# The first channel product of batches 6, 7 and of the tail chunk by seven block products in place of eight

## The chip, the cores and the metric

The kernel runs on one core of one Trainium2 chip. The metric is the device time of one launch in microseconds (us). "Before" is the kernel as it stands, "after" the kernel with the change below. Engines are named as the profile names them: PE (TensorE matmul), PEld (weight load of PE), DVE (VectorE), ACT (ScalarE), POOL (GpSimd), SP (SyncE, which here only issues DMAs).

## The reference

Attention by random features, then a mixer layer over its result; 8 batches of 576 rows and 512 channels:

```python
q_p, k_p = phi(q_s), phi(k_s)               # 8 heads, 128 features, exp
num = q_p @ (k_p^T v); den = q_p @ sum(k_p)
x   = num / den                             # [8, 576, 512]
h   = relu(x^T @ w_tok1) @ w_tok2           # over the 576 rows, 256 hidden
u   = x + h^T
out = u + relu(u @ w_ch1) @ w_ch2           # over the 512 channels, 1536 hidden
```

## The kernel before

Of each batch 512 rows are one block (c = 0 to 7); the 64 remaining rows of all eight batches are gathered into one more block of 512 rows, the tail chunk, c = 8 (`B`). A block passes through three stages. Attention (`attention`) makes the features, in four pairs of heads (hp = 0 to 3). Token mixing (`token_mix`) makes `u` and turns it by a DMA transpose issued by SP (L777) into `uT`, with the channels on the partitions; the tail chunk's `uTt` comes from four such transposes (L834). Channel mixing (`channel_mix`) multiplies `uT` by `w_ch1` (1536 hidden channels, twelve blocks `cb` of 128), applies relu into `r3`, and multiplies by `w_ch2`.

In the first channel product (L945) one block `cb` is four matmuls of 128x512 in one PSUM bank, one for each 128 input channels, and one relu of 128x512 on ACT or DVE (L268, L270) frees the bank. A block c has 48 such matmuls. The second product (`channel_out_fast`, L895) is done since batch 1 by Strassen's scheme in Winograd's form: the operands are cut into 2 x 2 quarters and seven products do the work of eight. It needs sums of quarters of `r3` (L273, eight per block, 128x768, on DVE) and sums of weights (L426, once); seven products O0 to O6 of twelve 128x256 matmuls write to three banks X, Y, Z; DVE reads them (L884) into the output tile `o` and adds `u`; two DMAs store it.

What runs when is written out by hand. Every piece of work is a job with a number. The list `ORDER` gives the order in which the jobs are issued; each engine takes its own jobs in that order, and waits only for what the job needs. `SLOT` says which of several equal buffers each job takes (the eight PSUM banks too): a job that takes a bank waits for the last reader of the bank's former content. `MOVED` sends a job to another engine than its usual one. The costs and keys of the jobs in the code do not enter a run.

Around the change the lists put work of two neighbouring batches between each other: while PE does the first channel product of batch 5, it also does attention of batch 6; the first product of 6 goes with attention and token mixing of 7; the first products of 7 and of the tail chunk stand together, with the second product of 7; the second product of the tail chunk ends the kernel.

The lines that the diff leaves alone but the prediction uses: L895 (matmuls of the second product), L945 (of the first), L884 (reads), L635, L647, L680, L713 (attention on PE), L722 and L723 (the attention result, two DVE instructions for each of eight heads), L659 (a DVE maximum).

## Time and profile before

| | |
|---|---|
| median of three runs | 281.75 us (281.57 to 281.98) |
| the profiled execution | 281.83 us, of which the span from the first to the last instruction is 280.0 us |
| granted TensorE clock, mean | 0.979 of full speed; 1.00 from 40 us on |
| PE busy | 267.5 us, 96% |
| DVE busy | 221.3 us, 79% |
| ACT busy | 141.1 us, 50% |
| POOL busy | 92.1 us, 33% |

Busy time is a share of the span. A matmul's own duration in the profile is longer than its distance from the next, because matmuls overlap in the array; the distance from start to start is what counts for the sum, and the chain view gives it (a piece of n matmuls, without the overlap of the last).

### The profile page before, as it was taken

How to read it: one execution, taken by the hardware profiler on the slowest of the kernel's cores; microseconds unless marked ns; L12 is line 12 of the kernel's file. 1: busy time of each engine (PE TensorE's matmuls, PEld its weight loads, DVE VectorE, ACT ScalarE, POOL GpSimd, SP SyncE). 2: the span in 40 equal slices, each digit the busy share in tenths (PEclk: the TensorE clock that was granted, in tenths of full speed). 3: DMA queues.
4: the chain of work that ended last, by engine and by line, in shares of the span. 5: the costliest groups of instructions: out<-in, count | busy, mean ns of one | idle time of the engine just before them, and what ended most of it. 6: DMA issues, size and time to landing. Idle time of an engine off the chain costs nothing.

```text
span 280.0 us, 6246 instructions
## 1 busy us (share of the span) xinstructions
PE 267.5 (96%) x2516; PEld 167.4 (60%) x2516; DVE 221.3 (79%) x457; ACT 141.1 (50%) x293; POOL 92.1 (33%) x116
## 2 busy tenths in 40 slices
PE   6579999999999999999999999999999999999993
PEld 2547545443657755665667546755675567456782
DVE  2598728499999799996997899977989595495583
ACT  2797993149676418743758445734764410033200
POOL 8587783007500971058008710510043000000001
PEclk9669999999999999999999999999999999999998
DMA  6999999999997999997989992960160324030125
GB/s 158 194 201 159 179 184 211 192 163 196 164 247 164 140 205 161 169 207 103 210 182 186 239 135 95 165 159 8 69 98 0 96 82 89 0 150 0 77 81 145
DMA packets 80524, 39.66 MB, mean 142 GB/s; under 512 B 63984, under 2 KB 76016, under 8 KB 80304
## 3 DMA queue, kind: packets, MB, share of 16 engines
q0 software_dynamic: 31744, 17.74, 44.2%
q1 hardware_dynamic: 46832, 15.77, 28.9%
q10 hardware_dynamic: 1920, 5.77, 5.5%
q8 instruction: 19, 0.31, 0.5%
q14 instruction: 9, 0.07, 0.1%
HBM read 35.95 MB, written 16.52 MB: 187 GB/s over the span
## 4 chain that ended last, share of the span: by engine, by line
PE 91%; DVE 4%; DMA 3%; SPq 0%; ACT 0%; issue 0%; DVEq 0%
PE bank L945 32%; PE bank L895 27%; PE bank L769 5%; PE bank L756 5%; PE bank L979 4%; PE bank L635 3%; DMA wc<-in_k_dram 3%; PE bank L647 3%; PE bank L713 3%; PE bank L680 2%; DVE km L659 1%; PE bank L823 1%; PE bank L795 1%; DVE kT L264 1%; PE bank L807 1%; PE bank L715 1%
## 5 line engine op out<-in xcount | busy, mean ns | idle before, releaser
L945 PE MATMUL bank<-uT,wc 128*128 128x512 f16 x376 | 90.0, 379 | 0.0
L268 ACT ACTIVATE r<-bank 128x512 f16<-128x512 f32 (+1 forms) x88 | 49.2, 603 | 81.0 <-PE bank L945 64.5
L273 POOL TENSOR_TENSOR vs<-v,vs 128x512 f16<-128x512 f16 x32 | 34.2, 1071 | 95.7 <-DVE vs L661 49.8
L945 PEld LDWEIGHTS <-wc 128*128 128x128 f16 x424 | 38.5, 98 | 38.8 <-issue 2.2
L493 ACT ACTIVATE qp<-bank 128x512 f16<-128x512 f32 x64 | 37.3, 627 | 8.8 <-PE bank L647 8.7
L895 PEld LDWEIGHTS <-r 128*128 128x128 f16 x384 | 36.7, 98 | 8.1 <-issue 1.0
L493 ACT ACTIVATE kp<-bank 128x512 f16<-128x512 f32 x64 | 36.7, 620 | 8.1 <-PE bank L635 8.1
L659 DVE TENSOR_REDUCE km<-kp 128x8 f16<-128x1024 f16 x32 | 38.6, 1206 | 0.6 <-ACT kp L493 0.4
L270 DVE TENSOR_SCALAR r<-bank 128x512 f16<-128x512 f32 (+1 forms) x38 | 24.9, 670 | 11.3 <-PE bank L945 6.7
L723 DVE TENSOR_TENSOR x<-bank,rc 128x320 f16<-128x320 f32 x62 | 30.5, 492 | 2.1
L895 PEld LDWEIGHTS <-S 128*128 128x128 f16 x288 | 28.0, 98 | 5.9 <-issue 0.4
L895 PE MATMUL bank<-T,r 128*128 128x256 f16 x192 | 23.8, 273 | 0.0
L895 PE MATMUL bank<-wc,r 128*128 128x256 f16 x192 | 23.6, 273 | 0.0
L895 PE MATMUL bank<-T,S 128*128 128x256 f16 x192 | 23.4, 273 | 0.0
L884 DVE TENSOR_TENSOR o<-u,bank 128x512 f32<-128x512 f16 x28 | 19.0, 678 | 4.5 <-PE bank L895 4.3
L884 DVE TENSOR_TENSOR o<-o,bank 128x512 f32<-128x512 f32 (+1 forms) x27 | 16.4, 618 | 7.6 <-PE bank L895 7.1
L924 POOL DMA_DIRECT2D out_dram<-o x2 | 1.3, 644 | 60.1 <-issue 60.1
L713 PEld LDWEIGHTS <-qp 128*128 128x128 f16 x256 | 13.7, 98 | 8.2 <-DVE kvsb L264 0.3
L772 DVE TENSOR_TENSOR u<-x,bank 128x512 f16<-128x512 f16 x28 | 17.7, 680 | 0.1
L713 PE MATMUL bank<-kvsb,qp 128*128 128x65 f16 x256 | 15.1, 193 | 0.1
L722 DVE RECIPROCAL rc<-bank 128x5 f32<-128x5 f32 x62 | 11.4, 184 | 4.2 <-PE bank L715 1.7
L769 PE MATMUL bank<-r,w 128*128 128x512 f16 x56 | 14.4, 381 | 0.0
(119 smaller groups left out, 378.9 us busy)
## 6 DMA issues: line engine op xcount, KB each, us to landing
out_dram<-o ACTq DMA_DIRECT2D x9, 512.0 KB, 2.7
q<-in_q_dram POOLq DMA_DIRECT2D x6, 576.0 KB, 9.7
wc<-in_moe_w_ch_dram POOLq DMA_DIRECT2D x4, 768.0 KB, 10.7
k<-in_k_dram POOLq DMA_DIRECT2D x6, 512.0 KB, 7.7
v<-in_v_dram POOLq DMA_DIRECT2D x6, 512.0 KB, 9.8
out_dram<-o SPq DMA_DIRECT2D x5, 512.0 KB, 4.8
r<-in_q_dram POOLq DMA_DIRECT2D x4, 288.0 KB, 6.7
v<-in_v_dram POOLq DMA_DIRECT2D x4, 256.0 KB, 8.7
```

Of the source, the lines that this page charges most:

```text
L268: nc.scalar.activation(out=out, in_=in_, func=AF.Relu)
L270: nc.vector.tensor_relu(out=out, in_=in_)
L273: (nc.gpsimd if eng == "POOL" else nc.vector).tensor_tensor(**kw)
L493: nc.scalar.activation(out=out, in_=in_, func=AF.Exp, bias=0.0, scale=1.0)
L659: nc.vector.reduce_max(out=mx, in_=kpv, axis=AX.X)
L713: nc.tensor.matmul(ps[:, k, j * 65 : (j + 1) * 65], st, s[:, i, 0 : D + 1], start=True, stop=True)
L723: nc.vector.tensor_tensor(out=t_x[place("x", b)][:, :, (2 * hp + hs[0]) * D : (2 * hp + hs[0] + n) * D].rearrange("p j (i d) -> p i j d", ...
L769: nc.tensor.matmul(ps, w2_of(tb, j), r1[:, tb, :], start=(tb == 0), stop=(tb == NT - 1))
L772: nc.vector.tensor_tensor(out=t_u[place("u", b)][:, j, :], in0=t_x[place("x", b)][:, j, :], in1=bank(n), op=ALU.add)
L884: nc.vector.tensor_tensor(out=o, in0=a, in1=ps, op=ALU.add)
L895: nc.tensor.matmul(ps[:, j * DH : (j + 1) * DH], a[:, cb, j * P : (j + 1) * P], w[:, cb, :], start=(bank_of(b, j0) not in held and j == j0 ...
L945: nc.tensor.matmul(ps, wc1[:, db, cb * P : (cb + 1) * P], moving(db), start=(db == 0), stop=(db == ND - 1))
```

## The change

For blocks 6, 7 and 8 (`FAST1 = 6`) the first channel product is done by the same seven-product scheme; `channel_in_fast` is new, and `channel_mix` calls it in place of the twelve plain blocks.

- The weights `wc1` are cut into quarters A11, A12, A21, A22; four sums of 128x1536 (named W.S1, W.S2, W.S4, W.S3 here) are made once, on DVE, in buffers of earlier batches; S3 overwrites A21.
- For each block four sums of 128x512 of quarters of `uT` (V1 to V4), on DVE.
- The hidden channels go in three pairs p = 0, 1, 2 of 128-blocks. For each pair there are seven products P1 to P7, each of four 128x256 matmuls into one of three banks X, Y, Z, and seven instructions of 128x512: `ka` copies X (after P1) into Y, so that P2 adds to it in PSUM; `y` is the relu of Y; `kb` and `kc` copy X after P6 and after P7 into 32-bit buffers in SBUF; `t22` (kc + Z after P5) and `t21` (kb + Z after P3) are sums on DVE into `r3`; `r` is the relu of X after P4. P2 and P6 need ka, P7 needs kb, P3 needs t22, P4 needs kc. Two quarters of `r3` then get their relu in place, in two parts each (1024 and 512 elements).
- In the second product of blocks 6 and 7 the read of X after O0 (DVE, adds `u`) becomes a copy of X into Y on ACT; O1 adds to it, and the read of Y adds `u`. The sums of `r3` come in parts of 128x1024 and 128x512 in place of two of 128x768.
- The lists: `ORDER` is as before up to the start of the first product of batch 5 (only the banks of some warm-up matmuls differ), and new from there. `SLOT` is new from the beginning, so that in the unchanged part of the order too the jobs take other banks. `MOVED` is new from job 727 on.

Read out job by job, the new list has PE at batch 5's first product (block C1 of batch b is b.C1) in this order: 6.kv@3, 7.kp@2, 7.kp@1, 7.kp@3, 6.kv@1, 6.n1@0, 5.C1.8, 6.n0@3, 6.n1@3, 5.C1.9, 5.C1.4, 6.n0@0, 6.n0@1, 5.C1.2, 6.n1@1, 5.C1.11, 7.kp@0, 7.kt, and then token mixing of 6 (kp, kt, kv, n are jobs of attention at L635, L530, L680 and L713, with the pair of heads behind @). DVE has meanwhile the eight results of batch 6's heads (L722, L723), with W.S1 after the second and W.S2 after the third; then five maxima of batch 7, four reads of token mixing, and W.S4 and W.S3 after them. The first products of batch 6 follow 5.O1, those of 7 follow 6.O0, and those of the tail chunk start after 6.O5, between the last products of 7. The last jobs of PE are 8.P4 of the three pairs and then the second product of the tail chunk alone.

```diff
--- before
+++ after
@@ ORDER (new from about its 880th entry on; up to there only the warm-up banks differ), SLOT (new throughout), MOVED (new from job 727) @@
...
@@ after MOVED @@
+FAST1 = 6
+def covered(name):
+    kind = name[0][0] if isinstance(name[0], tuple) else name[0]
+    if kind in ("X", "Y", "Z"):
+        return len(name) == 2
+    return kind in ("h2", "h3", "h4", "qp", "htt", "cX", "cY", "cZ") or kind == "h1" and name[1] > 0
+def seeded(name):
+    return name[0] == "cY" or name[0] == "Y" and len(name) == 2 and name[1] >= FAST1
@@ class Planner @@
         self.held = {}
+        self.whole = [False] * places["bank"]
...
                     assert i < self.places[tag] and not left.get(owner.get((tag, i)))
                     owner[tag, i] = (tag, name)
+                    if tag == "bank":
+                        assert self.whole[i] or not seeded(name)
+                        self.whole[i] = covered(name)
@@ shapes, homes and weight sums @@
+    A11, A21, A12, A22 = [wc1[:, 2 * k : 2 * k + 2, e * NH * P : (e + 1) * NH * P] for k in range(2) for e in range(2)]
+    S3 = A21
+    HOME = {1: "kT", 2: "qT", 4: "v"}
+    OF_V = {0: "kT", 1: "qT", 2: "v"}
+    def slot_of(tag):
+        t = {"kT": t_kT, "qT": t_qT, "v": t_v}[tag][place(tag, "W")]
+        return t if len(t.shape) == 2 else flat(t)
+    def S_of(n):
+        return S3 if n == 3 else slot_of(HOME[n])[:, 0 : 2 * NH * P].rearrange("p (k c) -> p k c", k=2)
+    def V_of(n):
+        return slot_of(OF_V[n])[:, 2 * NH * P : 2 * NH * P + 4 * P].rearrange("p (j k s) -> p j k s", j=2, k=2)
+    def s_of(c, p, x):
+        i = place("s", (c, p, x))
+        t = flat(t_r1[place("r1", "W")]) if i == 2 else flat(t_x[place("x", "W")])[:, 2 * SM * i : 2 * SM * (i + 1)]
+        return t.bitcast(FP32)
+    j_W = {}
+    def first_weights(plain):
+        for n, a, b, op in ((1, lambda: A21, lambda: A22, ALU.add), (2, lambda: S_of(1), lambda: A11, ALU.subtract),
+                            (4, lambda: A12, lambda: S_of(2), ALU.subtract), (3, lambda: A11, lambda: A21, ALU.subtract)):
+            e_w = "DVE"
+            def go_w1(n=n, a=a, b=b, op=op, e_w=e_w):
+                tt(e_w, out=S_of(n), in0=a(), in1=b(), op=op)
+            j_W[n] = add(e_w, 0.95, FAST1 - 0.2, go_w1, deps=[*j_wc1, *([j_W[n // 2]] if n in (2, 4) else [*j_W.values()]), *(plain if n == 3 else [])],
+                         take=[("x", "W"), ("r1", "W")] if n == 3 else [(HOME[n], "W")])
@@ channel_out_fast @@
-    def channel_out_fast(c, key, jr):
+    def channel_out_fast(c, key, jr, ready=None):
         def r3(i, e):
             return t_r3[place("r3", c)][:, NH * e : NH * e + NH, 2 * P * i : 2 * P * i + 2 * P]
         def s_of(i):
             return t_S[:, i - 1]
         sums = {}
-        for g in range(2):
-            part = slice(g * NH // 2, (g + 1) * NH // 2)
-            need = [jr[cb + NH * e] for cb in range(part.start, part.stop) for e in range(2)]
+        PARTS = (slice(0, 3), slice(3, 6)) if ready is None else (slice(0, 4), slice(4, NH))
+        if ready is None:
+            ready = {(i, e): [[jr[cb + NH * e] for cb in range(p.start, p.stop)] for p in PARTS] for i in range(2) for e in range(2)}
+        for g, part in enumerate(PARTS):
             steps = (
-                (1, lambda: (s_of(1), r3(1, 0), r3(1, 1)), ALU.add),
-                (3, lambda: (r3(1, 0), r3(0, 0), r3(1, 0)), ALU.subtract),
-                (2, lambda: (s_of(2), s_of(1), r3(0, 0)), ALU.subtract),
-                (4, lambda: (s_of(3), r3(0, 1), s_of(2)), ALU.subtract),
+                (1, lambda: (s_of(1), r3(1, 0), r3(1, 1)), ALU.add, [*ready[1, 0][g], *ready[1, 1][g]], ()),
+                (3, lambda: (r3(1, 0), r3(0, 0), r3(1, 0)), ALU.subtract, ready[0, 0][g], (1,)),
+                (2, lambda: (s_of(2), s_of(1), r3(0, 0)), ALU.subtract, ready[0, 0][g], (1,)),
+                (4, lambda: (s_of(3), r3(0, 1), s_of(2)), ALU.subtract, ready[0, 1][g], (2,)),
             )
+            if c < FAST1:
+                steps = tuple((i, what, op, [*ready[0, 0][g], *ready[0, 1][g], *need], after) for i, what, op, need, after in steps)
             prev = []
-            for k, (i, what, op) in enumerate(steps):
+            for k, (i, what, op, need, after) in enumerate(steps):
                 e_sum = "DVE"
-                def go(what=what, op=op, part=part, e_sum=e_sum, c=c, g=g, k=k):
+                def go_s(what=what, op=op, part=part, e_sum=e_sum, c=c):
                     o, a, b = what()
                     tt(e_sum, out=o[:, part], in0=a[:, part], in1=b[:, part], op=op)
-                job = add(e_sum, 0.5, key + KEYS["S"] + 0.1 * g + 0.01 * k, go, deps=[*need, *prev], take=[("S", c)])
+                job = add(e_sum, 0.5 if c < FAST1 else (0.61, 0.34)[g], key + KEYS["S"] + 0.1 * g + 0.01 * k, go_s,
+                          deps=[*need, *(prev if c < FAST1 else [sums[x][g] for x in after])], take=[("S", c)])
                 prev = [job]
                 sums.setdefault(i, []).append(job)
         ops = (
-            ("X", lambda: r3(0, 0), W11, []),
-            ("Y", lambda: r3(0, 1), W21, []),
+            ("X", lambda: r3(0, 0), W11, sum(ready[0, 0], [])),
+            ("Y", lambda: r3(0, 1), W21, sum(ready[0, 1], [])),
             ("X", lambda: s_of(2), T2, sums[2]),
             ("Z", lambda: s_of(1), T1, sums[1]),
             ("X", lambda: r3(1, 0), T3, sums[3]),
             ("Z", lambda: s_of(3), W22, sums[4]),
-            ("X", lambda: r3(1, 1), T4, sums[1]),
+            ("X", lambda: r3(1, 1), T4, [*sums[1], *sum(ready[1, 1], [])]),
         )
...
+        seed = c >= FAST1 and not tail
+        of_s = (2, 3, 4, 5, 6)
...
+                                             start=(bank_of(b, j0) not in held and j == j0 and cb == 0 and not (seed and k == 1)), stop=False, skip_group_check=True)
                     held[bank_of(b, j0)] = True
-                deps = [*need, *jr, *j_T, *j_wc2] + [outs[x, h] for x in ({2: ["sA"], 4: ["s2"], 5: ["22"], 6: ["s3"]}.get(k, []))]
...
+                if k == 0 and seed:
+                    e_a = engine("ACT", "DVE")
+                    def go_a(e_a=e_a):
+                        copy(e_a, bank(bank_of("Y", 0)), bank(bank_of("X", 0)))
+                    outs["sA", h] = add(e_a, 0.5, key + KEYS["c2"], go_a, deps=[j], take=[("bank", bank_of("Y", 0))])
+                elif k == 0:
                     outs["sA", h] = read(k, "X", 0, 0, True, [j], False, j0, j1)
                 elif k == 1:
-                    outs["11", h] = read(k, "Y", 0, 0, False, [j, outs["sA", h]], True, j0, j1)
+                    outs["11", h] = read(k, "Y", 0, 0, seed, [j, outs["sA", h]], True, j0, j1)
@@ new: channel_in_fast @@
+    plain = []
+    def channel_in_fast(c, key, jt):
+        def src():
+            return t_uT[place("uT", c)] if c < B else uTt
+        def u_of(k, i):
+            return src()[:, 2 * i : 2 * i + 2, 2 * k : 2 * k + 2, :]
+        v_of = V_of
+        own = [("uT", c)] if c < B else []
+        sums = {}
+        for n, what, op, after in (
+            (1, lambda: (v_of(0), u_of(0, 1), u_of(0, 0)), ALU.subtract, ()),
+            (2, lambda: (v_of(1), u_of(1, 1), v_of(0)), ALU.subtract, (1,)),
+            (4, lambda: (v_of(2), u_of(1, 0), v_of(1)), ALU.subtract, (2,)),
+            (3, lambda: (u_of(0, 1), u_of(1, 1), u_of(0, 1)), ALU.subtract, (1,)),
+        ):
+            e_sum = "DVE"
+            def go_u(what=what, op=op, e_sum=e_sum):
+                o, a, b = what()
+                tt(e_sum, out=o, in0=a, in1=b, op=op)
+            sums[n] = add(e_sum, 1.0, key - 0.2, go_u, deps=[*jt, *[sums[x] for x in after], *j_W.values()], take=[("V", c)], give=own)
+        ops = {
+            1: ("X", lambda: A11, lambda: u_of(0, 0), [], True), 2: ("Y", lambda: A12, lambda: u_of(1, 0), [], False),
+            6: ("X", lambda: S_of(2), lambda: v_of(1), [sums[2], j_W[2]], False), 5: ("Z", lambda: S_of(1), lambda: v_of(0), [sums[1], j_W[1]], True),
+            7: ("X", lambda: S3, lambda: u_of(0, 1), [sums[3], j_W[3]], False), 3: ("Z", lambda: S_of(4), lambda: u_of(1, 1), [j_W[4]], False),
+            4: ("X", lambda: A22, lambda: v_of(2), [sums[4]], False),
+        }
+        raw = {(i, e): [] for i in range(2) for e in range(2)}
+        for p in range(NH // 2):
+            at = key + 0.15 * p
+            def bank_of(b, p=p):
+                return ("c" + b, c, p)
+            def rows(i, e, p=p):
+                return t_r3[place("r3", c)][:, NH * e + 2 * p : NH * e + 2 * p + 2, 2 * P * i : 2 * P * i + 2 * P]
+            def seen(b, bank_of=bank_of):
+                return bank(bank_of(b)).rearrange("p (t s) -> p t s", t=2)
+            def product(n, deps, give=(), p=p, bank_of=bank_of, at=at):
+                b, a, moving, need, begin = ops[n]
+                def go_p(b=b, a=a, moving=moving, begin=begin):
+                    ps, m, a_ = bank(bank_of(b)), moving(), a()
+                    for t in range(2):
+                        cb = 2 * p + t
+                        for k in range(2):
+                            nc.tensor.matmul(ps[:, 2 * P * t : 2 * P * t + 2 * P], a_[:, k, cb * P : (cb + 1) * P], m[:, :, k, :],
+                                             start=(begin and t == 0 and k == 0), stop=False, skip_group_check=True)
+                j = add("PE", mm(4, 256), at, go_p, deps=[*jt, *j_wc1, *need, *deps], take=[("bank", bank_of(b)), ("r3", c)],
+                        give=[*([("V", c)] if n in (4, 5, 6) else own), *[(x, "W") for x in (*HOME.values(), "x", "r1")], *give])
+                j.heavy = True
+                return j
+            def kept(x, deps, give=(), p=p, seen=seen, at=at):
+                e_k = engine("ACT", "DVE")
+                def go_k():
+                    copy(e_k, s_of(c, p, x).rearrange("p (t s) -> p t s", t=2), seen("X"))
+                return add(e_k, 0.5, at, go_k, deps=deps, take=[("s", (c, p, x))], give=give)
+            def summed(x, b, i, e, deps, free, p=p, seen=seen, rows=rows, at=at, bank_of=bank_of):
+                def go_t():
+                    nc.vector.tensor_tensor(out=rows(i, e), in0=s_of(c, p, x).rearrange("p (t s) -> p t s", t=2), in1=seen(b), op=ALU.add)
+                j = add("DVE", 0.6, at, go_t, deps=deps, give=[("s", (c, p, x))] + ([("bank", bank_of(b))] if free else []))
+                raw[i, e].append(j)
+                return j
+            p1 = product(1, [])
+            e_a = engine("ACT", "DVE")
+            def go_a(e_a=e_a, bank_of=bank_of):
+                copy(e_a, bank(bank_of("Y")), bank(bank_of("X")))
+            ka = add(e_a, 0.5, at, go_a, deps=[p1], take=[("bank", bank_of("Y"))])
+            p2 = product(2, [ka])
+            p5 = product(5, [])
+            e_y = engine("ACT", "DVE")
+            def go_y(e_y=e_y, rows=rows, seen=seen):
+                relu_to(e_y, rows(0, 0), seen("Y"))
+            raw[0, 0].append(add(e_y, 0.5, at, go_y, deps=[p2], give=[("bank", bank_of("Y"))]))
+            p6 = product(6, [ka])
+            kb = kept("b", [p6])
+            p7 = product(7, [kb])
+            kc = kept("c", [p7])
+            t22 = summed("c", "Z", 1, 1, [kc, p5], False)
+            p3 = product(3, [t22])
+            summed("b", "Z", 1, 0, [kb, p3], True)
+            p4 = product(4, [kc])
+            e_r = engine("ACT", "DVE")
+            def go_r(e_r=e_r, rows=rows, seen=seen):
+                relu_to(e_r, rows(0, 1), seen("X"))
+            raw[0, 1].append(add(e_r, 0.5, at, go_r, deps=[p4], give=[("bank", bank_of("X"))]))
+        ready = {k: [raw[k][:2], raw[k][2:]] for k in ((0, 0), (0, 1))}
+        for i, e in ((1, 1), (1, 0)):
+            ready[i, e] = []
+            for g, part in enumerate((slice(0, 4), slice(4, NH))):
+                e_p = engine("DVE", "ACT")
+                def go_n(part=part, i=i, e=e, e_p=e_p):
+                    x = t_r3[place("r3", c)][:, NH * e + part.start : NH * e + part.stop, 2 * P * i : 2 * P * i + 2 * P]
+                    relu_to(e_p, x, x)
+                ready[i, e].append([add(e_p, (0.33, 0.2)[g], key + 0.4, go_n, deps=raw[i, e][2 * g : 2 * g + 2])])
+        return ready
@@ channel_mix @@
     def channel_mix(c, key, jt):
+        if c == FAST1:
+            first_weights(plain)
+        if c >= FAST1:
+            channel_out_fast(c, key, [], channel_in_fast(c, key, jt))
+            return
```

More of the change, by code (lines that the diff above doesn't have):

```diff
@@ L87, in key_of, with __init__ @@
     return NEAR.get(str(b), {}).get(name, KEYS[name])
+class Job:
+    def __init__(self, eng, cost, key, fn, deps, take, give, rows, wire):
+        self.eng, self.cost, self.key, self.fn = eng, cost, key, fn
+        self.deps, self.take, self.give = deps, take, give
+        self.rows, self.wire = rows, wire
+        self.end = None
+        self.heavy = False
+FAST1 = 6
[6 more added lines that the diff above has]
+    return name[0] == "cY" or name[0] == "Y" and len(name) == 2 and name[1] >= FAST1
 class Job:
@@ L123, in run @@
                 self.warm(-1 - n)
+                self.whole[-1 - n] = True
                 continue
@@ L139, in place, with engine @@
         return self.held[tag, name]
-    def engine(self, usual):
+    def engine(self, usual, *others):
         return MOVED.get(len(self.jobs), usual)
@@ L192 @@
     COUNT = {"qT": 3, "kT": 3, "v": 3, "vt": 2, "qp": 4, "kp": 4, "vs": 4, "qpt": 2, "kpt": 2, "vbd": 2,
[L193 removed]
+             "kvsb": 3, "ktt": 2, "x": 3, "r1": 3, "u": 3, "uT": 3, "r3": 2, "S": 1, "V": 1, "s": 3, "o": 2, "bank": 8}
     plan = Planner(COUNT)
@@ L694, in attention @@
                        give=[("kp", (b, hp)), ("vs", (b, hp)), ("kpt", b)] + ([("vbd", b)] if dma_in else []))
-            e_kv = engine("ACT" if b >= NPE or BY[("ko", "ko1")[b]][hp] == "A" else "DVE")
+            e_kv = engine(*("ACT", "DVE") if b >= NPE or BY[("ko", "ko1")[b]][hp] == "A" else ("DVE", "ACT"))
             def kv_out(hp=hp, n_kv=n_kv, e_kv=e_kv):
```

26 lines of the change are left out of this document (12 added, 14 removed), and 47 rows, old and new, of the table ORDER.

## Prediction

> **What bounds the kernel now.** I read the page first: its busy shares, and its chain of work that ended last.
>
> ```profile
> PE 267.5 (96%) x2516; PEld 167.4 (60%) x2516; DVE 221.3 (79%) x457; ACT 141.1 (50%) x293; POOL 92.1 (33%) x116
> ...
> PE 91%; DVE 4%; DMA 3%; SPq 0%; ACT 0%; issue 0%; DVEq 0%
> ...
> L945 PEld LDWEIGHTS <-wc 128*128 128x128 f16 x424 | 38.5, 98 | 38.8 <-issue 2.2
> ```
>
> PE is busy for 96% of the span and makes 91% of the chain. A busy share can hide waits, so I asked the windows view for the stretch that the change rewrites, from 178 us to PE's end.
>
> ```profile
> 178.00:275.60 97.60, 97.56 (x798) 63.90 (x795) 74.45 (x148) 33.03 (x66) 10.06 (x11) 1.00 0.28 74
> ```
>
> PE is busy for 97.56 of 97.60 us at full clock; DVE for 74.45, ACT for 33.03. So this stretch lasts as long as its matmuls, and less matmul time shortens it, if DVE and ACT keep pace. What a matmul costs is in the chain view (start, length, what).
>
> ```profile
> 237.37 13.81 PE bank L945 x64
> ...
> 265.08 10.49 PE bank L895 x96
> 275.60 0.42 DVE o L884
> ```
>
> 64 matmuls of 512 columns without a gap: 13.81/64 = 0.2158 us each. 96 of 256 columns: 10.49/96 = 0.1093 us each. A weight load takes 0.098 us (its row is above), less than the 0.1093 us, and lies beneath the matmul before it; so a doubled number of loads per column shows no cost in L895, which already works like this.
>
> **The matmuls removed.** A block had 48 matmuls of 512 columns, 48 x 0.2158 = 10.36 us. Now it has 3 pairs x 7 products x 4 = 84 matmuls of 256, 84 x 0.1093 = 9.18 us. Three blocks: 3 x 1.18 = **-3.55 us** on PE, which is the path. The weight loads go from 48 to 84 a block, hidden as said.
>
> **What DVE and ACT get.** Prices come from DVE's and ACT's groups, kept apart by shape (count, busy us, mean ns).
>
> ```profile
> L270 DVE TENSOR_SCALAR r<-bank 128x512 f16<-128x512 f32 x36 | 24.1, 683 | 10.5 <-PE bank L945 6.7 <-PE bank L756 3.5
> ...
> L884 DVE TENSOR_TENSOR o<-o,bank 128x512 f32<-128x512 f32 x21 | 14.0, 676 | 7.1 <-PE bank L895 6.6 <-issue 0.2
> ...
> L273 DVE TENSOR_TENSOR S<-S,r 128x768 f16<-128x768 f16 x16 | 8.8, 551 | 0.0
> ...
> L609 DVE COPY qpt<-qpt 128x512 f16<-128x512 f16 x1 | 0.3, 294 | 0.0
> ```
> ```profile
> L264 ACT COPY o<-bank 128x512 f32<-128x512 f32 x2 | 1.2, 604 | 1.4 <-PE bank L979 1.4
> ```
>
> And the weight sums for the second product, in DVE's timeline, with POOL's beside them:
>
> ```profile
> 55.70 0.95 DVE L426 TENSOR_TENSOR T<-wc 128x1536 f16<-128x1536 f16 x1
> 56.57 2.47 DVE L772 TENSOR_TENSOR u<-x,bank 128x512 f16<-128x512 f16 x4
> ...
> 64.55 1.81 DVE L426 TENSOR_TENSOR T<-wc 128x1536 f16<-128x1536 f16 x1
> ```
> ```profile
> 64.07 1.47 POOL L273 TENSOR_TENSOR vs<-v,vs 128x512 f16<-128x512 f16 x1
> ```
>
> Instructions overlap by a little, so the distance counts: four of L772 in 2.47 us with a length of 0.68 are 0.60 apart, and the sum at 55.70 is followed after 0.87. DVE gains, in the stretch: four W sums at 0.87 = 3.5; twelve V sums of 128x512, two thirds of the 0.551 of 128x768, 0.36 each = 4.3; eighteen t sums like `o<-o,bank`, at 0.60 = 10.8; eight copies or relus of the new scheme that MOVED gives to DVE, 4.8; eight of the twelve in-place relus. The trace has no such relu: the nearest row is the 16-bit copy of 512 in 0.294, the upper bound a two-operand sum at 0.36 for 512; so 0.3 for 512 and 0.6 for 1024, together 3.6, between 3.3 and 4.6. DVE loses sixteen plain relus (9.6) and two reads after O0 (1.2). Sum: +16.2, so 90.7 of some 94 us. DVE becomes nearly as full as PE. ACT has 55 of the new copies and relus and of batch 5's relus, at 0.604, where it had 32 relus: 33.03 + 23 x 0.604 = 47 of 94 us.
>
> [...]
>
> **What PE waits for.** I walked the new list from the point where it departs, with these prices, engine by engine. The first tight place is token mixing of batch 6, which needs all eight results of its heads. DVE there:
>
> ```profile
> 183.26 0.68 DVE L270 TENSOR_SCALAR r<-bank 128x512 f16<-128x512 f32 x1
> ```
> ```profile
> 189.37 0.19 DVE L722 RECIPROCAL rc<-bank 128x5 f32<-128x5 f32 x1
> ...
> 190.00 0.18 DVE L722 RECIPROCAL rc<-bank 128x5 f32<-128x5 f32 x1
> ```
>
> At 183.26 DVE comes to this part of the list in both versions; the relu of that row goes to ACT, and from there eight results at 0.63 (189.37 to 190.00) and two W sums at 0.87 end at 183.26 + 5.04 + 1.74 = 190.04. PE:
>
> ```profile
> 182.26 0.41 PE L680 MATMUL bank<-vs,kp 128*128 128x65 f16 x8
> ...
> 182.56 0.28 PE L713 MATMUL bank<-kvsb,qp 128*128 128x65 f16 x4
> ...
> 182.71 0.28 PE L713 MATMUL bank<-kvsb,qp 128*128 128x65 f16 x4
> ```
> ```profile
> 194.18 0.33 PE bank L635 x8
> ```
>
> From 182.26 it has five column blocks at 0.863, eight n at 0.15 (182.56 to 182.71), two kv at 0.30 (182.26 to 182.56), four kp at 0.33, and kt with half of that: 4.32 + 1.20 + 0.60 + 1.32 + 0.16 = 7.6, so 189.86. PE waits 0.2, with the hand-over **+0.3 us**. What is queued behind token mixing on PE (blocks of batch 5) waits with it.
>
> After that DVE runs without a pause to about 213 us and PE reaches each of its needs with little to spare. V1 and P1 of batch 6 need `uT`; its transpose is issued at 199.5 behind the last read of token mixing, and lands by
>
> ```profile
> DMA to landing us min/median/max: 4.3/5.3/5.7
> ```
>
> 205.2 at the latest; PE comes to 6.P1 at 205.3 to 205.5. One n of batch 7 finds its bank free 0.3 late; 5.O4 has its read 0.4 before PE is there, 7's token mixing its results 0.5 before. From 7.P1 on DVE has pauses again, and the slacks are 0.2 to 0.5: V3 and kb before 7.P7 (0.1), t22 before P3 (0.4), the copy in place of the read after O0 (0.60, with 0.06 for the hand-over) before O1 under three products, 3 x 0.437 = 1.31. The output buffers come free by stores with
>
> ```profile
> out_dram<-o SPq DMA_DIRECT2D x5, 512.0 KB, 4.8
> ```
>
> and 6's read of Y stands about there: up to 0.3 late. For these I take **+0.3 us** (nothing to 0.8).
>
> The new SLOT lets jobs of the unchanged part take banks nearer to their last reader. The reader's end before is set against PE's start, pair by pair. The worst is at 39.76, where a kv takes the bank that this exp leaves at 39.87:
>
> ```profile
> 39.12 0.75 ACT L493 ACTIVATE qpt<-bank 128x512 f16<-128x512 f32 x1
> ```
> ```profile
> 39.76 0.41 PE L680 MATMUL bank<-vs,kp 128*128 128x65 f16 x8
> ```
>
> That is 0.11, with 0.06 for the hand-over 0.17; ten others are below 0.15 and partly take the same shift: **+0.2 us** (0.1 to 0.5).
>
> **The sum.** PE's end: 275.60 - 3.55 + 0.3 + 0.3 + 0.2 = 272.85. After it the last read and store as before, 280.0 - 275.6 = 4.4: a span of 277.25. The profiled execution has 281.83 - 280.0 = 1.83 around its span, and lies 0.08 above the median of the runs: 277.25 + 1.83 - 0.08 = **279.0 us**, 2.75 less. What a measurement of this kernel can tell from no change is about 0.2%, 0.56 us.
>
> **Rivals.** (1) *DVE becomes the bound between 183 and 213 us.* For it: 90.7 of 94 us, and a first stretch without a pause. The W sums are its price: the row at 64.55 took 1.81 where that at 55.70 took 0.95, and POOL's sum at 64.07 ran beside it. If two of the four fall on one, 1.9 us go to PE: 280.9. Against it: in POOL's timeline the sums of batch 6 run before the W sums,
>
> ```profile
> 182.94 1.05 POOL L273 TENSOR_TENSOR vs<-v,vs 128x512 f16<-128x512 f16 x1 [0.93 <-PE bank L715]
> ```
>
> ending at 183.99, W.S1 beginning at 184.5. [...] Chance 0.15.
>
> (2) *Slower: the products wait for their copies.* 45 products (five of each of nine pairs) now need a read of their own bank, where a column block needed only a free bank. One copy is 0.604 with 0.06; between a product and the one that needs its copy the list has two products at least, 0.87, so a copy that starts at once is hidden, one that stands behind another on ACT or DVE isn't. If 45 products wait 0.1 us more each, that is 4.5 us: 283.5. It decides from 2.75/45 = 0.061 us on average. Against it: ACT is at half of its time, and the pairs are interleaved. Chance 0.12.
>
> (3) *The whole gain:* no wait of PE is new: 281.75 - 3.55 = 278.2. For it: before, PE has next to none. Chance 0.10.
>
> **How the numbers follow.** The forecast has 0.63 (278.2 to 279.9 by its bounds), rival 1 0.15 (279.9 to 281.5), rival 2 0.12, rival 3 0.10. The range 277.9 to 281.5 leaves out rival 2 and the far ends of the others. Faster by over 0.2%: 0.63 + 0.10 + most of rival 1 = 0.84; same: 0.05; slower: 0.11.
>
> **What would show it.** PE matmuls 2516 + 108 = 2624; 252 of 256 columns in the first product, 0.109 apart, and no group of 512 columns after batch 5's. DVE near 90 us busy from 178 us on. PE's idle time before token mixing of 6 at 0.3 us, ended by the head's result (L723). PE's end at 272.9 and 4.4 us after it. I'm wrong if products start more than 0.12 apart, if W sums take 1.8, or if idle times of PE ended by ka, kb or t22 add up to over 1 us.

## The result, and the profile after

The changed kernel takes 279.76 us (median of four runs, 279.37 to 279.81), the kernel before beside it 281.77 us: a ratio of 0.9926 with a 95% interval of 0.9908 to 0.9943. The gain is 2.0 us; 279.0 us, a gain of 2.75, was forecast. The profiled execution of the changed kernel has 279.72 us and a span of 277.9. Its page, first the engines, then the shares of the chain:

```profile
PE 265.6 (96%) x2624; PEld 179.5 (65%) x2624; DVE 233.7 (84%) x487; ACT 154.5 (56%) x318; POOL 91.6 (33%) x115
...
PE 88%; DVE 4%; DMA 3%; ACT 2%; issue 1%; ACTq 0%; DVEq 0%
```

The windows view of the rewritten stretch (start and end; its length; PE, PEld, DVE, ACT, POOL busy):

```profile
178.00:273.50 95.50, 94.65 (x908) 74.85 (x906) 86.93 (x178) 46.54 (x91) 9.51 (x10) 1.00 0.28 77
```

PE has 2624 matmuls, as worked out, but for the first time it is idle: 94.65 of 95.50 us, where before it was 97.56 of 97.60. DVE stands at 86.93 us, ACT at 46.54. Three pieces of the chain:

```profile
231.57 3.50 PE bank L1053 x32
...
264.34 9.21 PE bank L965 x84
273.57 0.42 DVE o L954
```

The new products run at 3.50/32 = 0.1094 us a matmul, like those of the second product (9.21/84 = 0.1096). PE ends at 273.57 where it ended at 275.60, 2.03 sooner, and what follows takes 4.4 us, as before. So the saving of 3.55 was there, and 1.5 of it was lost in waits. The waits view of PE from 178 us on lists three and no more (who waited for whom, us, times, longest); before, it lists none:

```profile
PE bank L965 <- DVE o L954: 0.5, 1, 0.5
PE bank L699 <- DVE x L787: 0.2, 1, 0.2
PE bank L1053 <- ACT bank L297: 0.2, 1, 0.2
```

PE's idle time counts there from the modelled end of a matmul, which lies behind its distance to the next: a 256-column matmul lasts 0.273 us and the next starts after 0.109 (512 columns: 0.379 and 0.216), so each bracket of one is 0.16 too small, and for the short matmuls of L699 it is 0.2. From start to start PE lost 0.43 us ahead of 7.kp@3, 0.32 ahead of 6.P6/1 and 0.61 ahead of 5.O5. Here they are in the timelines, in order of time, each with the instruction that it waits for (start, length, instruction, idle time before it):

```profile
183.54 0.49 DVE L787 TENSOR_TENSOR x<-bank,rc 128x320 f16<-128x320 f32 x1
184.09 0.40 PE L699 MATMUL bank<-omT,kT 64*128 64x128 f16 x8 [0.24 <-DVE x L787]
...
208.02 0.68 DVE L954 TENSOR_TENSOR o<-o,bank 128x512 f32<-128x512 f32 x1
208.73 0.57 ACT L297 COPY bank<-bank 128x512 f32<-128x512 f32 x1 [1.57 <-DVE o L954]
209.35 0.49 PE L1053 MATMUL bank<-qT 128*128 128x256 f16 x3 [0.16 <-ACT bank L297]
...
223.62 1.02 DVE L306 TENSOR_TENSOR S<-r,S 128x768 f16<-128x768 f16 x2
224.56 0.68 DVE L954 TENSOR_TENSOR o<-o,bank 128x512 f32<-128x512 f32 x1
225.29 0.38 PE L965 MATMUL bank<-wc,S 128*128 128x256 f16 x2 [0.45 <-DVE o L954]
```

From the end of a DVE or ACT instruction here to the start of what waits for it are 0.03 to 0.06 us; the forecast took 0.06 for the hand-over. First: 7.kp@3 takes the bank of 6.n1@2, whose result, the first of batch 6's eight, DVE reads until 184.04. Second: 6.ka/1 on ACT, idle for 1.57 us, waits for the bank that DVE reads in 5.r11 until 208.70, and 6.P6/1 waits for 6.ka/1; 5.r11 stands on DVE behind the new sums V1 and V2 of batch 6. Third: 5.O5 adds to the bank that 5.r22 reads, and 5.r22 stands on DVE behind the last two sums of batch 5 (5.s4). All three are ended by DVE, which runs without a pause around the second, from 199.6 to 210.3. The fourth loss is in the unchanged part of the order, between two attention products of batch 6 (PE's timeline, before and then after):

```profile
176.54 0.60 PE L647 MATMUL bank<-qT,omT 64*128 64x512 f16 x4
176.98 0.39 PE L635 MATMUL bank<-omT,kT 64*128 64x128 f16 x8
```
```profile
176.60 0.81 PE L711 MATMUL bank<-qT,omT 64*128 64x512 f16 x4
177.24 0.40 PE L699 MATMUL bank<-omT,kT 64*128 64x128 f16 x8
```

The four matmuls hold 0.64 us where they held 0.44: 0.20 lost between the second and the third, with other banks in the same order. What else stands between PE's matmuls are gaps of about 0.1 us (0.09 to 0.12), nearly all where the tile shape changes, mostly from 128 to 64 rows or back; they add up to 1.81 us before and 1.70 after. So -3.55 + 0.43 + 0.32 + 0.61 + 0.20 - 0.11 = -2.10, and the stretch from 176.5 us on is 2.09 shorter (below).

### The profile page after: what moved, and what is told of

Its sections match the earlier page's. It is cut to its first block, busy times and chain, and to the rows that moved or that the text cites. A ratio compares the mean times of both kernels' runs of the same rounds, so it can differ in the third digit from the quotient of the medians.

```text
span 277.9 us, 6547 instructions
## 1 busy us (share of the span) xinstructions
PE 265.6 (96%) x2624; PEld 179.5 (65%) x2624; DVE 233.7 (84%) x487; ACT 154.5 (56%) x318; POOL 91.6 (33%) x115
## 4 chain that ended last, share of the span: by engine, by line
PE 88%; DVE 4%; DMA 3%; ACT 2%; issue 1%; ACTq 0%; DVEq 0%
PE bank L965 25%; PE bank L1120 22%; PE bank L1053 9%; PE bank L833 5%; PE bank L820 5%; PE bank L1155 4%; PE bank L711 3%; PE bank L699 3%; DMA wc<-in_k_dram 3%; PE bank L777 3%; PE bank L744 2%; DVE o L954 1%; PE bank L887 1%; DVE x L787 1%; PE bank L859 1%; ACT qp L557 1%
## 5 line engine op out<-in xcount | busy, mean ns | idle before, releaser
L301 ACT ACTIVATE r<-bank 128x512 f16<-128x512 f32 (+1 forms) x82 | 46.3, 604 | 43.5 <-PE bank L1120 25.6
L1120 PE MATMUL bank<-uT,wc 128*128 128x512 f16 x280 | 67.9, 379 | 0.0
L557 ACT ACTIVATE qp<-bank 128x512 f16<-128x512 f32 x64 | 36.6, 624 | 8.0 <-PE bank L711 5.2
L723 DVE TENSOR_REDUCE km<-kp 128x8 f16<-128x1024 f16 x32 | 38.5, 1205 | 0.6 <-ACT kp L557 0.4
L999 POOL DMA_DIRECT2D out_dram<-o x1 | 0.7, 665 | 73.4 <-issue 73.4
L303 DVE TENSOR_SCALAR r<-bank 128x512 f16<-128x512 f32 (+1 forms) x26 | 17.1, 663 | 7.5 <-PE bank L820 4.9
L954 DVE TENSOR_TENSOR o<-u,bank 128x512 f32<-128x512 f16 x28 | 19.0, 679 | 2.8 <-PE bank L965 2.6
L954 DVE TENSOR_TENSOR o<-o,bank 128x512 f32<-128x512 f32 (+1 forms) x25 | 15.1, 612 | 2.7 <-PE bank L965 2.5
L711 PE MATMUL bank<-qT,omT 64*128 64x512 f16 x64 | 12.5, 410 | 1.7 <-ACT qT L297 1.7
```

What stands on the lines that cost most here:

```text
L301: nc.scalar.activation(out=out, in_=in_, func=AF.Relu)
L557: nc.scalar.activation(out=out, in_=in_, func=AF.Exp, bias=0.0, scale=1.0)
L711: nc.tensor.matmul(ps[e], omT[half[e]], t[half[e], 2 * hp : 2 * hp + 2, 0:R], start=True, stop=True)
L723: nc.vector.reduce_max(out=mx, in_=kpv, axis=AX.X)
L954: nc.vector.tensor_tensor(out=o, in0=a, in1=ps, op=ALU.add)
L1120: nc.tensor.matmul(ps, wc1[:, db, cb * P : (cb + 1) * P], moving(db), start=(db == 0), stop=(db == ND - 1))
```

## The experiments

Two theories stand against each other. *Local stalls*: PE is the bound, and DVE's order delays it in three places. *DVE is the bound*: its sum of work sets the end, the stalls are where this shows, and a new order only moves them. The first 176 us of a run shift by up to 0.4 us either way from run to run (the stretch starts between 176.02 and 176.76), so next to the median stands the stretch in the profiled execution from the first matmul of L711 (L647 before) after 176 us to the start of the last read (L954, L884); it agrees between two executions of the changed kernel to 0.01. Names of jobs stand beside the numbers in the diffs.

| run | median us | ratio to before, 95% | stretch us |
|---|---|---|---|
| before | 281.77 | | 99.06 |
| after | 279.76 | 0.9926 [0.9908, 0.9943] | 96.97 |
| e0, the change again | 279.34 | 0.9921 [0.9905, 0.9937] | 96.98 |
| e1, 5.s4 early | 278.96 | 0.9910 [0.9891, 0.9929] | 96.37 |
| e2, 5.r11 early | 279.84 | 0.9939 [0.9923, 0.9955] | 97.20 |
| e3, 7.kp@3 and two W sums late | 282.54 | 1.0032 [1.0016, 1.0048] | 100.02 |
| e4, no W sums | 279.24 | 0.9909 [0.9887, 0.9931] | 96.67 |
| e5, V sums on GpSimd | 281.49 | 0.9985 [0.9972, 0.9998] | 98.44 |
| e6, an eighth left out, no sums | 279.88 | 0.9934 [0.9911, 0.9956] | 96.85 |
| e7, 5.s4 and W.S4 late | 278.90 | 0.9898 [0.9877, 0.9919] | 96.41 |
| e8, 5.s4, V sums of 6 and 8 on GpSimd | 278.70 | 0.9902 [0.9886, 0.9918] | 96.05 |
| e9, another bank for 7.kp@3 | 279.47 | 0.9935 [0.9916, 0.9954] | 97.15 |
| e10, e8 and e9, W.S1 and W.S2 on GpSimd | 278.53 | 0.9888 [0.9874, 0.9902] | 95.72 |

The kernel before had medians of 281.56, 281.82 and 281.60 us beside e0 to e3, e4 to e7 and e8 to e10. The intervals of neighbours overlap; the small differences are read from the stretch and the stalls. A stretch is one execution, though, and it shows more than the medians: e1, e8 and e10 are 0.61, 0.93 and 1.26 us below e0 in the stretch and 0.38, 0.64 and 0.81 us in the median.

**e0, the change again.**

> The changed kernel once more, beside the three re-ordered ones, so that steps of 0.3 us can be read on one chip. Both theories: 279.76 us within 0.2, a gain of 2.0 on the kernel before. In the trace three stalls of TensorE that the kernel before has not: 0.43 us ahead of 7.kp@3 (184.1), 0.32 ahead of 6.P6/1 (209.4), 0.61 ahead of 5.O5 (225.3), and 0.20 ahead of 6.qp@1 (177.0). With 0.1 at changes of the tile shape all gaps after 176 add up to 3.26 us, against 1.81 before: 3.55 saved less 1.45 is the gain of 2.0 to 2.1.

279.34 us, 0.2 below what was expected, with before lower by 0.2 too. The three stalls are there with the same lengths.

**e1, the third stall.**

```diff
 ORDER
-..., 957, 968 (6.t22/0), 1101, 980, ..., 1003, 848 (5.s4g1), 861, 858 (5.r22), ...
+..., 957, 968 (6.t22/0), 844 (5.s4g0), 848 (5.s4g1), 1101, 980, ..., 1003, 861, 858 (5.r22), ...
```

> Same work; batch 5's two fourth sums (s4, 0.55 us each) are put on VectorE ahead of 6.t22/1, into its idle time at 214.2, and so no longer stand ahead of 5.r22, for which 5.O5 waits. Theory of local stalls (TensorE is the bound, three places of VectorE's order hold it up): 5.r22 starts at the end of 5.O3, some 0.9 us sooner, the 0.61 us ahead of 5.O5 shrink to 0.1, nothing behind it is late: 279.2 us (279.1 to 279.4). Rival (VectorE's sum of work is the bound, its order is not): the stall comes back elsewhere, 279.75 within 0.2.

```profile
214.02 1.02 DVE L306 TENSOR_TENSOR S<-r,S 128x768 f16<-128x768 f16 x2
...
223.49 0.69 DVE L954 TENSOR_TENSOR o<-o,bank 128x512 f32<-128x512 f32 x1
```

In DVE's timeline the two sums stand in the former pause, 5.r22 starts at 223.49 and not at 224.56, and 5.O5 has no idle time before it. The stretch is 0.61 shorter, just the stall: local stalls hold here. The median, 278.96 us, lies 0.14 below the expected range.

**e2, the second stall by order.**

```diff
 ORDER
+..., 716, 852 (5.r11), 973, 1072 (7.no1@1), 1100 (7.no1@3), 727, 959, 955 (6.V1), 853, 960 (6.ka/0), 974 (6.ka/1), ..., 975 (6.P2/1), 964 (6.P6/0), ...
-..., 956 (6.V2), 852 (5.r11), ..., 974 (6.ka/1), ..., 964 (6.P6/0), ..., 978 (6.P6/1), 965, 1056, 975 (6.P2/1), ...
```

> Same work; 5.r11 (0.68 us on VectorE, frees the bank that 6.ka/1 fills) goes ahead of 7.no1@1, 7.no1@3 ahead of 6.V1, and 6.P2/1 ahead of 6.P6/0 on TensorE, so that V2 has 0.4 us more. Local stalls: the 0.32 us ahead of 6.P6/1 go, nothing new waits: 279.45 us (279.35 to 279.6). Rival, VectorE full from 178 to 210: the wait moves to 6.P6/0 for V2 or to 7.n0@2 for its bank, 279.75 within 0.2.

```profile
209.74 0.49 DVE L787 TENSOR_TENSOR x<-bank,rc 128x320 f16<-128x320 f32 x1
210.29 0.28 PE L777 MATMUL bank<-kvsb,qp 128*128 128x65 f16 x4 [0.32 <-DVE x L787]
```

The 0.32 us are gone, and 0.48 stand ahead of 7.n1@0, whose bank DVE reads until 210.23: the stretch grows by 0.22. The rival is right at this place, though the new wait is none of those that it named. DVE has no pause here, and this order only moved the wait.

**e3, the first stall by order.**

```diff
 ORDER
-..., 1087 (7.kp@3), 903 (6.kv@1), 1089, 951 (W.S1), 893 (6.n1@0), 827 (5.C1.8), ..., 952 (W.S2), ...
+..., 903 (6.kv@1), 827 (5.C1.8), 893 (6.n1@0), 1087 (7.kp@3), 1089, ..., 1093 (7.km@3), 951 (W.S1), ..., 952 (W.S2), 953 (W.S4), ...
```

> Same work; on TensorE 7.kp@3, which waited 0.43 us for a bank, goes behind 6.kv@1, 5.C1.8 and 6.n1@0, and W.S1 and W.S2 (0.95 us each) leave VectorE's queue ahead of the last head results of batch 6: S1 behind 7.km@3, S2 ahead of W.S4. Local stalls: token mixing of batch 6 starts 0.3 to 0.4 us sooner (190.2 for 190.57) and the end follows: 279.4 us (279.3 to 279.6). Rival: with VectorE's work only put off, the 0.4 us come back at 6.P6/0 or 6.P6/1, where VectorE is late already: 279.75 within 0.2, with a gap ahead of 6.P6/1 of 0.7.

```profile
186.47 0.28 PE L777 MATMUL bank<-kvsb,qp 128*128 128x65 f16 x4 [0.69 <-ACT kp L557]
...
210.92 0.68 DVE L954 TENSOR_TENSOR o<-o,bank 128x512 f32<-128x512 f32 x1
211.63 0.57 ACT L297 COPY bank<-bank 128x512 f32<-128x512 f32 x1 [1.89 <-DVE o L954]
212.26 0.49 PE L1053 MATMUL bank<-qT 128*128 128x256 f16 x3 [0.60 <-ACT bank L297]
```

Both were wrong, 3.2 us slower. The edit was bad in itself: a kp that comes 1.3 us later has its exp later, and 6.n0@3 waits 0.88 us (from start to start) for that bank. The last rows fit the rival's part: with the W sums put off, the stall ahead of 6.P6/1 is 0.77 us, as it said (0.7). Six more waits of 0.2 to 0.4 us from start to start came up, which were not taken apart.

**e4, without the sums of the weights.**

```diff
             def go_w1(n=n, a=a, b=b, op=op, e_w=e_w):
-                tt(e_w, out=S_of(n), in0=a(), in1=b(), op=op)
+                pass
```

> The changed kernel with the four sums of the weights left out (3.8 us of VectorE, S1 and S2 at 184.6 and 186.1, S4 and S3 at 200.1 and 200.9); the products read what lies in their places. It prices the terms of 0.3 us for token mixing of batch 6, and tells whether VectorE's work bounds the kernel. Theory of local stalls: 7.kp@3 still waits 0.43 us (6.no1@2 stands ahead of the sums), token mixing of 6 starts where it did, only the 0.32 us ahead of 6.P6/1 go: 279.0 to 279.1 where the change had 279.34 in the last call. Rival, VectorE's work is the bound between 178 and 210: 1 us or more comes back: 278.3 or less.

PE's waits:

```profile
PE bank L965 <- DVE o L954: 0.5, 1, 0.5
PE bank L699 <- DVE x L787: 0.2, 1, 0.2
```

3.8 us less on DVE give PE 0.3: the stretch is 0.31 shorter than in e0. The median, 279.24 us, is above the expected range, and far from the rival's. The stall ahead of 6.P6/1 is gone, the others stay. So the sums cost what one stall costs; DVE's sum of work isn't the bound of the whole stretch, and the stall ahead of 7.kp@3 is not of their making.

**e5, the V sums on GpSimd.**

```diff
-            e_sum = "DVE"
+            e_sum = "POOL"
             def go_u(what=what, op=op, e_sum=e_sum):
```

> The changed kernel with the twelve V sums of batches 6, 7 and the tail (128x512, 0.42 us on VectorE) on GpSimd, where such a sum takes 1.07 us in the profile of before. Theory (each V chain is 1.9 us longer, VectorE has 4.2 us less): 6.P6/0 late by 0.4 to 0.9, 7.P5/2 by 0.1, 8.P6/0 by 0.9, less the 0.32 us that 6.P6/1 waited: 0.5 to 1.5 us slower than the change, 280 to 281. Rival 1 of the prediction (VectorE's sums that run beside GpSimd's take twice as long, 1.8 for 0.95 us, as the T sums did): several us, 282 or more. If VectorE's sum of work were the bound: faster, 278 to 279.

DVE in the changed kernel beside the same jobs of batch 7:

```profile
229.40 0.49 DVE L303 TENSOR_SCALAR r<-r 128x512 f16<-128x512 f16 x2
229.92 0.42 DVE L306 TENSOR_TENSOR S<-r 128x512 f16<-128x512 f16 x1
230.26 0.42 DVE L303 TENSOR_SCALAR r<-r 128x1024 f16<-128x1024 f16 x1
```

With the V sums on GpSimd, DVE, GpSimd's two of these and PE behind them:

```profile
228.57 1.46 DVE L303 TENSOR_SCALAR r<-r 128x512 f16<-128x512 f16 x2
230.06 1.33 DVE L306 TENSOR_TENSOR S<-r 128x512 f16<-128x512 f16 x1
231.31 1.37 DVE L303 TENSOR_SCALAR r<-r 128x1024 f16<-128x1024 f16 x1
...
229.95 1.15 POOL L306 TENSOR_TENSOR v<-uT,qT 128x512 f16<-128x512 f16 x1
231.06 1.33 POOL L306 TENSOR_TENSOR uT<-uT 128x512 f16<-128x512 f16 x1
...
234.78 0.38 PE L1053 MATMUL bank<-uT,wc 128*128 128x256 f16 x2 [1.62 <-ACT bank L297]
```

Four DVE instructions that take 1.33 us together (0.49 + 0.42 + 0.42) take 4.16; the last three end 0.15 to 0.3 us after a sum of GpSimd ends. 6.s1g0 and 6.r11 come later by that, 7.ka/0 with them, and PE waits 1.78 us from start to start; with the stall ahead of 6.P6/1 gone, the stretch is 1.46 longer. 281.49 lies between the theory and rival 1: the price is rival 1's, but PE pays it in one batch of three. In the tail one relu of 128x512 takes 1.21 us too, beside V4 (246.89 to 248.05), and PE isn't late:

```profile
246.99 1.21 DVE L303 TENSOR_SCALAR r<-r 128x512 f16<-128x512 f16 x1
```

Around the V sums of batch 6 DVE reads PSUM, and its reads and head results keep 0.68 and 0.49 us (DVE, then GpSimd):

```profile
205.68 0.68 DVE L954 TENSOR_TENSOR o<-o,bank 128x512 f32<-128x512 f32 x1
...
206.49 0.49 DVE L787 TENSOR_TENSOR x<-bank,rc 128x320 f16<-128x320 f32 x1
...
205.64 1.16 POOL L306 TENSOR_TENSOR qT<-uT,kT 128x512 f16<-128x512 f16 x1
206.75 1.16 POOL L306 TENSOR_TENSOR uT<-uT 128x512 f16<-128x512 f16 x1
```

The relus of batch 7, with one input, grew about as much as the sum with two (0.42 to 1.37 and 0.42 to 1.33 us); by what mechanism, the runs don't show.

**e6, the saving without its price.** The kernel before, 18 of 144 matmuls left out.

```diff
-                for db in range(ND):
-                    nc.tensor.matmul(ps, ..., start=(db == 0), stop=(db == ND - 1))
+                nd = ND - 1 if c >= 6 and cb % 2 else ND
+                for db in range(nd):
+                    nc.tensor.matmul(ps, ..., start=(db == 0), stop=(db == nd - 1))
```

> The kernel before with the last of the four matmuls left out in every second column block of the first product of batches 6, 7 and the tail: 18 of 144, an eighth of 128x512, and no sums at all. It is the saving without its price. If TensorE bounds all of the last third: 18 x 0.2158 = 3.88 us less, 281.6 - 3.9 = 277.7 (277.5 to 278.0). Rival: relus and bank turnover take over in part when the four matmuls of a block become three: 278.5 or more.

```profile
215.72 0.28 PE L713 MATMUL bank<-kvsb,qp 128*128 128x65 f16 x4 [0.58 <-DVE kvsb L264]
...
251.88 0.50 PE L895 MATMUL bank<-T,S 128*128 128x256 f16 x3 [0.76 <-DVE S L273]
```

The rival's time is right; what PE waits for is a cast and a sum on DVE, not a relu or a bank itself. Of 3.88 us the stretch keeps 99.06 - 96.85 = 2.21: two waits for DVE, 0.75 and 0.92 us from start to start, come up in a kernel whose PE had been idle for 0.04 us of 97.60. This order feeds PE just in time and has hardly any slack; a faster PE alone runs into the engine that fed it. Ahead of both waits DVE runs with hardly a pause, from 212.7 to 215.7 and from 247.5 to 251.8; whether its load there or the place of the two jobs in its queue decides, this run doesn't tell.

**e7, work put off into the pause.** W.S4 goes with 5.s4; W.S3 and the V sums wait only for the sum that they need.

```diff
 ORDER
-..., 950, 1095, 824, 953 (W.S4), 1090, ..., 856, 1070, 957 (6.V4), 968 (6.t22/0), 1101, ..., 844, 1003, 848, 861, ...
+..., 950, 1095, 824, 1090, ..., 856, 1070, 953 (W.S4), 957 (6.V4), 968 (6.t22/0), 844, 848, 1101, ..., 1003, 861, ...
-... [j_W[n // 2]] if n in (2, 4) else [*j_W.values()] ...
+... [j_W[n // 2]] if n in (2, 4) else [j_W[1]] if n == 3 else [] ...
-... deps=[*jt, *[sums[x] for x in after], *j_W.values()] ...
+... deps=[*jt, *[sums[x] for x in after], *([j_W[n]] if n != 3 else [])] ...
```

> The changed kernel, same work: batch 5's fourth sums into VectorE's idle time at 214 as in the run before, and W.S4 too, from 200.1 to just ahead of 6.V4 (213.2), with the V sums waiting only for the weights' sum whose place they share. VectorE's full stretch ahead of 6.P6/1 is 0.87 us shorter. Local stalls: both the 0.61 us ahead of 5.O5 and the 0.32 ahead of 6.P6/1 go: 278.4 (278.2 to 278.6), 0.5 to 0.9 less than the change. Rival: work that is put off on VectorE comes back as a wait at 6.P4/1, 6.P7/1 or 6.P3/0 between 214 and 219: 279.0 or more.

```profile
216.12 0.70 DVE L297 COPY bank<-bank 128x512 f32<-128x512 f32 x1
216.87 0.60 PE L1053 MATMUL bank<-qT 128*128 128x256 f16 x4 [0.21 <-DVE bank L297]
```

Both stalls are gone, and a new one of 0.37 us stands ahead of 6.P6/2, for whose copy 6.ka/2 DVE comes too late. The stretch, 96.41, is that of e1 (96.37), and 278.90 us lies between the two forecasts. The rival is right in kind: the work that was put off comes back between 214 and 219, at a product that it did not name. The pause at 214 has no room for both.

**e8, the V sums of 6 and of the tail on GpSimd.** e1's order, and

```diff
-            e_sum = "DVE"
+            e_sum = "DVE" if c == 7 else "POOL"
             def go_u(what=what, op=op, e_sum=e_sum):
```

> The changed kernel with batch 5's fourth sums moved to 214 (as before), and the V sums of batch 6 and of the tail on GpSimd, those of batch 7 on VectorE. In the run with all twelve on GpSimd a stall of 1.78 us came up in batch 7 alone, where VectorE's in-place relus and S sums took 1.2 to 1.4 us beside GpSimd for 0.28 to 0.42; beside the V sums of 6 VectorE reads PSUM and was not slower. Theory (the price is the doubling of VectorE's SBUF work, and it falls where such work stands beside GpSimd): no stall in batch 7, none ahead of 6.P6/1 or 5.O5: 0.9 us below the change, 278.3 to 278.6. Rival (GpSimd's sums themselves are late, 1.15 us against 0.42): the stall of 0.4 to 0.9 ahead of 6.P6/0 or 8.P6/0, 279.0 or more.

```profile
PE bank L699 <- DVE x L787: 0.2, 1, 0.2
```

One wait is left. The stretch is 0.93 shorter than the change's, the two stalls' sum (0.32 + 0.61); GpSimd's sums, 1.15 to 1.2 us each, are not late. Here too one relu in the tail takes 1.21 us beside V4, and PE doesn't wait for it. The median, 278.70 us, is 0.1 above the expected range.

**e9 and e10, the first stall.** In e9 banks 5 and 6 change names in `SLOT` from 7.kp@3 on, and

```diff
 ORDER
-..., 1089, 951, 893 (6.n1@0), 827 (5.C1.8), ...
+..., 1089, 951, 827 (5.C1.8), 893 (6.n1@0), ...
```

> The changed kernel, same work: from 7.kp@3 on banks 5 and 6 change names, so that 7.kp@3 takes the bank that 5.relu3 has left at 183.3 and not the one of 6.n1@2, and 5.C1.8 goes ahead of 6.n1@0, whose bank comes free at 184.7. W.S1 and W.S2 stay in VectorE's queue ahead of the last head results of batch 6. Local stalls: the 0.43 us go, 279.05 (278.95 to 279.15 where the change has 279.34). Rival (the prediction's own term: eight head results and two sums end at 190.0 to 190.2 on VectorE, whatever TensorE does): TensorE waits 0.3 us ahead of 6.t1t, or ahead of 6.P6/1 more than 0.32, and the time is that of the change within 0.15.

In e10 both edits of e9, e8's, and

```diff
-            e_w = "DVE"
+            e_w = "POOL" if n < 3 else "DVE"
```

> The bank exchange of the run beside it with W.S1 and W.S2 on GpSimd (T sums of twice their size took 1.9 us there, so both end by 188 to 189, long ahead of their products at 207), batch 5's fourth sums at 214, V sums of 6 and the tail on GpSimd. VectorE then has nothing but head results ahead of token mixing of 6. Both theories: the 0.43 us ahead of 7.kp@3 go and token mixing of 6 starts 0.3 sooner: 278.1 (277.9 to 278.3), the lowest of all. If GpSimd's sums slow the head results beside them: 278.5 or more.

e9: the last head result of batch 6 on DVE, token mixing (L813) behind it on PE, and later the product that waits for 6.ka/1:

```profile
189.56 0.49 DVE L787 TENSOR_TENSOR x<-bank,rc 128x320 f16<-128x320 f32 x1
190.18 0.41 PE L813 MATMUL bank<-x,w1t 64*128 64x512 f16 x2
...
209.24 0.49 PE L1053 MATMUL bank<-qT 128*128 128x256 f16 x3 [0.24 <-ACT bank L297]
```

e9 gains nothing (97.15; 279.47 us, as the rival said): the 0.43 us come back as 0.13 at 6.kv@1, which waits for GpSimd's product, 0.28 at 6.n0@1, whose bank's reader stands behind W.S2 on DVE, about 0.1 at token mixing, and 0.08 more ahead of 6.P6/1 (0.40). With the two sums on GpSimd,

```profile
183.44 3.10 POOL L306 TENSOR_TENSOR kT<-wc 128x1536 f16<-128x1536 f16 x1
186.62 3.09 POOL L306 TENSOR_TENSOR qT<-kT,wc 128x1536 f16<-128x1536 f16 x1
...
189.51 0.38 PE L813 MATMUL bank<-x,w1t 64*128 64x512 f16 x2
```

of the 0.43 only 0.13 are left, token mixing starts at 189.51 for 190.18 (0.28 of it is the shift ahead of the stretch), and PE's waits view is empty. So two causes lay over each other, the bank and DVE's queue; taking either away alone (e4, e9) gains nothing there, taking both 0.33 (96.05 to 95.72). e10 takes 278.53 us, 0.9888 of before, and its stretch is 3.34 shorter than before's: nearly the whole 3.55. Its interval lies below before's and the change's. It still misses its expected range by 0.2 us and stands at the edge of the other case, but the head results beside GpSimd's sums keep their 0.49 us. The profiled execution has 277.88 us, with the earliest start of the stretch of all runs (176.02); the other three take 278.51 to 278.71. The two sums ended at 189.7 and not by 188 to 189: the T sums that priced them are of 128x1024, two thirds of their size and not twice.

## Why the prediction was right

The mechanism holds: PE is the path, it saves what its matmuls cost, and waits for DVE take part of it back. 279.76 us lies in the range and near the upper end of the forecast's own part (278.2 to 279.9); 2.0 of 2.75 us came.

**The saving** is right to the matmul: 0.1094 us each, and 3.34 of 3.55 where the waits are taken away (e10). (3 x 1.18 is 3.54; the 0.01 changes nothing.)

**Token mixing of 6, +0.3.** Near in size, 0.43, but by another cause: not at token mixing behind the eighth head result and the two W sums, but 6 us ahead of it, in a bank that the first of the eight results frees, before any W sum. That the size fits is in part luck. e9 shows that a wait of the forecast's kind stood right behind it: without the bank, DVE's queue with W.S2 takes the time back.

**Later small waits, +0.3 (0 to 0.8).** This is the term that was mis-sized: 0.32 + 0.61 = 0.93, above its upper bound, and with the 0.43 for 0.3 it is the miss of 0.7 us at PE's end (272.85 forecast, 273.57 found). The walk listed nine candidates (uT, n's bank, 5.O4, 7's token mixing, kb, t22, the copy after O0, V3, 6's read of Y), and PE waits for none of them; the two that are late were not on the list. Both are reads of batch 5 on DVE: r11 stands behind V1 and V2, new sums, and r22 behind batch 5's own s4. The walk followed the new operations and some old ones, but not every read that frees a bank of PE.

**Banks in the unchanged part, +0.2.** The pair that the forecast called the worst does wait, by the 0.17 that it gave: in the changed kernel's trace PE's seven matmuls from 38.19 on, 0.216 apart, are through at 39.70, and the kv starts at 39.87, where before (from 38.25 to 39.76) it followed without a gap. Another 0.20, not named, stands between two attention products of 6. That makes 0.37, within the bounds (0.1 to 0.5). Where the stretch starts (176.60 for 176.54) the first of them can't be seen, as this start shifts by more from run to run; the smaller gaps at changes of the tile shape gave 0.11 back.

**DVE, 90.7 us.** It has 86.93: the +16.2 were 12.5. The in-place relus, priced at 0.3 and 0.6, are the clearest part:

```profile
L303 DVE TENSOR_SCALAR r<-r 128x1024 f16<-128x1024 f16 x4 | 1.7, 419 | 0.0
...
L303 DVE TENSOR_SCALAR r<-r 128x512 f16<-128x512 f16 x4 | 1.1, 286 | 0.0
```

From start to start they are 0.34 (230.26 to 230.60, where the next sum starts) and 0.20 (two in 0.49): 2.2 us for eight and not 3.6. (The upper bound should have been 4.3 and not 4.6, by its own 0.36.) That is 1.4 of the 3.7 us; the rest was not broken down. The row of the copy was right as a length (0.294 for 0.286); the forecast took the length for the distance, and doubled it for 1024, where the length only grows to 0.419.

**Rival 1** (DVE the bound, W sums at 1.81): its price did not fall due, the four W sums take 0.948 to 0.952 us, and GpSimd runs nothing beside them (from 184.07 to 191.75 and from 198.5 on). e5 shows that the price is real (0.42 to 1.33 us for a sum). **Rival 2** (products wait for their copies) needed 0.061 us at each of 45 products; all of PE's waits for copies are one of 0.32, 0.007 each. **Rival 3** (the whole gain, 278.2) was not in this list's reach; e10, with eight V sums and two W sums on GpSimd, another bank and another order, comes to 278.53.

## What to carry to other kernels

When an order written out by hand gets a faster step, look for the gain's leak not at the new instructions alone: here all three waits were for old reads on DVE, one behind new sums, one behind an old sum and one in a bank taken too soon. So list each of PE's banks with its last reader's place in that queue. A wait can hide a second one: take both away before you judge either. In this kernel sums within SBUF could go to GpSimd where VectorE reads PSUM, and not where VectorE has sums or relus within SBUF that PE waits for (the stretch was 96.05 us in e8 for 96.37 in e1, and 98.44 in e5 for the change's 96.97).
